# Half of w_v goes through DRAM, the other half is narrowed in place with its steps spread out

## The chip, the cores and the metric

The kernel runs on one core of one Trainium2 chip. The time is device time in microseconds (us). The engines are named as the profile names them: PE is TensorE, DVE is VectorE, ACT is ScalarE, POOL is GpSimd, SP is SyncE, whose queue starts most transfers. Three runs of the kernel before took 486.54, 487.22 and 488.26 us; the median is 487.22 us.

## The reference

Three layers follow one another on 2 x 768 tokens of width 512: a retention layer (attention with decay), a mixture of eight experts, and a channel mix. What bears on the change is the last layer and its weights:

```python
def _moe2_ref(x, mu_k, mu_r, w_k, w_v, w_r):
    x_prev = np.concatenate([np.zeros((B, 1, D), dtype=np.float32), x[:, :-1, :]], axis=1)
    xk = mu_k * x + (1.0 - mu_k) * x_prev
    xr = mu_r * x + (1.0 - mu_r) * x_prev
    k = np.maximum(xk @ w_k, 0.0)
    v = k * k @ w_v
    r = 1.0 / (1.0 + np.exp(-(xr @ w_r)))
    return (r * v).astype(np.float32)

    # the inputs: np.sqrt gives a float64 scalar, so the products are float64
    'w_k': np.random.randn(d_model, d_ff).astype(np.float32) * (1.0 / np.sqrt(d_model)),
    'w_v': np.random.randn(d_ff, d_model).astype(np.float32) * (1.0 / np.sqrt(d_ff)),
    'w_r': np.random.randn(d_model, d_model).astype(np.float32) * (1.0 / np.sqrt(d_model))
```

w_k, w_v and w_r reach the kernel as 64-bit floats. The engines work on 32 bits, so the kernel narrows each of them with integer and float operations on the two 32-bit words of each number.

## The kernel before

Every matrix product is made of three: each operand x is cut into a high part (ACT copies it to the rounded type) and a low part (DVE subtracts the high part from x), and `split3` adds high x high, high x low and low x high. So each weight costs one ACT instruction and one DVE instruction before PE can use it (`w_split`, lines 145 to 159).

The kernel has three phases. The retention layer and the routing of tokens come first. Then a loop over the eight experts: `up` (four column groups fp, PE, then ACT and DVE make the parts of the hidden activations hh and hl), `flip` (inputs of the next expert), `down` (two halves of 128 tokens each). After each of four groups of `up` and four of `down` a side function `side_w` runs; its calls are numbered c = 0 to 63, eight per expert. The last expert's second half is `down_last`. Last comes the channel mix over six groups n of 256 tokens: `k_part(n)` (the product with w_k in four groups fp, then relu, square and the parts k2h, k2l), `r_part(n)` (the product with w_r and the sigmoid), `v_part(n)` (the product with w_v, eight row blocks f for each half t of the tokens). In the text, the groups of `k_part` are called fp0 to fp3.

All engines run their own instruction list in the order in which this Python code issues instructions; an instruction that waits holds everything behind it on its engine, the SP queue of transfers too.

`pieces` (lines 122 to 133) is the list of weight pieces in the order of use. A piece is loaded into one of four buffers `raw` by `w_load` when an earlier piece is finished, and cut into parts by `w_split` about four calls later.

The 64-bit weights take one of two ways:

- `narrow` (line 738): for w_k and w_r. Twelve parts of 128 x 512 numbers are read, narrowed in three steps and written to DRAM as 32-bit floats (`wk32`, `wr32`), and later loaded and cut like any other weight. Step one is `narrow_1` (two DVE instructions), step two `narrow_2` (two), step three `narrow_3` (two); before them ACT takes the magnitude (line 723). One step runs at each call of `side_w` for which line 950 lets it. The list `written` holds the write back until the next call.
- `direct` (line 773): for w_v. Its eight row blocks j are loaded as pieces of kind "d", narrowed in the same three steps, and cut at once into the high part (ACT, line 807) and the low part (DVE, line 786). Its steps run from call c = 56 on, up to three places in `k_part(0)`, then in `r_part(0)` and in `k_part(1)` (two steps after each group). `t`, the buffer of the magnitude, exists once.

`first_k` (line 1106) also makes the inputs of group 1 after fp2: `weigh(1)` on ACT scales the rows, `fetch(1)` transposes them on PE and copies them on ACT (line 1020), `mix(1, 0)` blends them on ACT and DVE (lines 913, 917, 925, 926) for `k_part(1)`; after `r_part(0)`, `mix(1, 1)` makes the same for `r_part(1)`.

Of the kernel before, what the change touches and what calls it, by code (L numbers as in the profile page):

```python
# [10 lines left out]
F32 = mybir.dt.float32  # L11
# [5 lines left out]
ALU = mybir.AluOpType  # L17
# [4 lines left out]
P = 128  # L22
B, H, S, D = 2, 8, 768, 64
DM = H * D
NE, FF = 8, 1024
# [4 lines left out]
ND = DM // P  # L30
NF = FF // P
# [13 lines left out]
def kernel(  # L45
# [16 lines left out]
    act, dve, pool, pe, sp = nc.scalar, nc.vector, nc.gpsimd, nc.tensor, nc.sync  # L62
# [6 lines left out]
    dp = ctx.enter_context(tc.tile_pool(name="dp", bufs=1, space=DRAM))  # L69
# [38 lines left out]

    wk32 = dp.tile([P, ND, FF], F32, name="wk32")
    wr32 = dp.tile([P, ND, DM], F32, name="wr32")
    wpools = [wp1, wp1]

    def w_tiles(kind, i, n, f):
        pl, bufs = (wp1, 2) if kind == "w1" else (wpools[i % 2], 1)
        if (kind, i) == ("w1", NE + 1):
            n *= 2
        return [pl.tile([P, n, f], F32R, name=f"{kind}{x}{i}", tag=f"{kind}{x}", bufs=bufs) for x in "hl"]

    W = {}
    plan = []
    for e in range(NE):
        plan += [("w1", e, w1[e], ND, FF), ("w2", e, w2[e], NF, DM)]
    plan += [("w1", NE, wk32, ND, FF), ("w1", NE + 1, wr32, ND, DM)]
    PIECE = 1024
    pieces = []
    for kind, i, src, n, f in plan:
        m = PIECE // f
        if i == NE + 1:  # L130
            pieces += [("d", NE, wv, NF, DM, j, 1) for j in range(2)]
        pieces += [(kind, i, src, n, f, j, m) for j in range(0, n, m)]
    pieces += [("d", NE, wv, NF, DM, j, 1) for j in range(2, NF)]
    staged = {}
    at = [0, 0]

    def w_load():
        if at[0] < len(pieces):
            kind, i, src, n, f, j, m = pieces[at[0]]
            t = stp.tile([P, m, f], mybir.dt.int64 if kind == "d" else F32, name=f"raw{at[0]}", tag="raw")  # L140
            sp.dma_start(out=t, in_=src[:, j : j + m, :])
            staged[at[0]] = t
            at[0] += 1
# [473 lines left out]
    with ExitStack() as bctx:  # L617
# [120 lines left out]
        def narrow():  # L738

            n = DM  # L740
            parts = []
            for src, dst in ((wk, wk32), (wr, wr32)):
                sv, dv = (x.rearrange("p a b -> p (a b)") for x in (src, dst))
                parts += [(sv[:, j : j + n], dv[:, j : j + n]) for j in range(0, sv.shape[1], n)]
            raws, ts = {}, {}

            def read(k):
                if k < len(parts):
                    raws[k] = bp.tile([P, n], mybir.dt.int64, name=f"raw64_{k}", tag="raw64")
                    sp.dma_start(out=raws[k], in_=parts[k][0])  # L750

            def begin(k):
                if k < len(parts):
                    ts[k] = tp.tile([P, n], I32, name="t1", tag="t1")
                    magnitude(raws[k], ts[k])

            read(0)
            read(1)
            yield
            begin(0)  # L760
            for k in range(len(parts)):
                t2 = tp.tile([P, n], I32, name="t2", tag="t2")
                narrow_1(ts[k])
                yield
                narrow_2(raws[k], ts[k], t2, ts[k])
                yield
                narrow_3(raws[k], ts[k].bitcast(F32), ts[k].bitcast(F32), t2, t2.bitcast(F32))
                written.append(lambda t=t2, k=k: sp.dma_start(out=parts[k][1], in_=t.bitcast(F32)))
                begin(k + 1)
                read(k + 2)  # L770
                yield

        def direct():

            hi, lo = W["w2", NE] = w_tiles("w2", NE, NF, DM)
            todo = [i for i, x in enumerate(pieces) if x[0] == "d"]
            raws, ts = {}, {}
            split = None

            def begin(i):  # L780
                raws[i] = staged.pop(i).rearrange("p a b -> p (a b)")
                ts[i] = tp.tile([P, DM], I32, name="t", tag="t", bufs=1)
                magnitude(raws[i], ts[i])

            def finish(h, l, x):
                dve.tensor_tensor(out=l, in0=x, in1=h.bitcast(F32), op=ALU.subtract)  # L786
                w_load()

            begin(todo[0])
            yield  # L790
            for k, i in enumerate(todo):
                while at[1] < i:
                    w_split()
                    yield
                raw, t = raws[i], ts[i]
                low, high = (raw.bitcast(F32).rearrange("p (n t) -> p n t", t=2)[:, :, x] for x in range(2))
                h, l = (x[:, pieces[i][5], :] for x in (hi, lo))
                narrow_1(t)
                if split:
                    finish(*split)  # L800
                yield

                narrow_2(raw, t, t, high.bitcast(I32))
                yield
                narrow_3(raw, high, low, t, high)
                at[1] += 1
                act.copy(out=h, in_=high)  # L807
                split = h, l, high
                if k + 1 < len(todo):
                    begin(todo[k + 1])  # L810
                yield
            finish(*split)

        conv = narrow()
        perm = bp.tile([P, 2, 2 * P], F32R, name="perm", bufs=1)
# [126 lines left out]
        tail = direct()  # L942

        def side_w():
            c = calls[0]
            calls[0] += 1
            late = list(written)
            if c < 56:
                w_split(1 if c > 1 else 2)
            if c == 2 or (c >= 4 and c % 8 not in (3, 7)):  # L950
                next(conv, None)
            if c >= 56:
                for _ in range((2, 2, 2, 1, 1, 1, 2, 2)[c - 56]):
                    next(tail)
            for w in late:
                w()
            del written[: len(late)]
# [15 lines left out]
    with ExitStack() as mctx:  # L973
# [6 lines left out]
        todo = [(b, g) for b in range(B) for g in range(NG)]  # L980
# [128 lines left out]
        def first_k(fp):  # L1109
            if fp == 0:  # L1110
                mix_first(1, 1)
                x_new(1)
                for a in range(2):
                    act.copy(out=xt[1][:, 2 * a : 2 * a + 2, 0:1], in_=px[1 + a][:, :, GS - 1 : GS])
            else:
                next(tail, None)
            if fp == 1:
                weigh(1)
            if fp == 2:
                fetch(1)  # L1120
                xk[1] = mix(1, 0)
                read(2)

        def two(_):
            for _ in range(2):
                next(tail, None)


        xk, xr = {0: x0[0]}, {}
# [1 line left out]
        pk = k_begin(xk[0])  # L1131
        xr[0] = x0[1]
        k_part(0, xk[0], pk, first_k)
        r_part(0, xr[0], two)
        xr[1] = mix(1, 1)
        k_part(1, xk[1], {}, two)
        for _ in tail:
            pass
        for n in range(1, NN):
# [63 lines left out]
```

## Time and profile before

| | |
|---|---|
| median of three runs | 487.22 us |
| the profiled execution: its time | 489.27 us |
| the profiled execution: its span | 487.5 us |
| PE busy | 453.8 us (93% of the span) |
| DVE busy | 315.7 us (65%) |
| ACT busy | 220.1 us (45%) |
| moved by DMA | 81.86 MB, mean 168 GB/s |

The span runs from the first to the last instruction; the time of the execution is 1.8 us longer. A busy PE is not PE at its peak: PE can be busy at the lower of its two clocks. The line PEclk of the page gives, in 40 slices of the span (12.2 us each), the clock that was granted, in tenths of full speed.

### The profile page before, as it was taken

What the parts mean: (1) busy time and instruction counts of PE and PEld (TensorE: products, weight loads), DVE (VectorE), ACT (ScalarE), POOL (GpSimd) and SP (SyncE); (2) the same over time, 40 slices, a digit from 0 to 9 for tenths busy, and PEclk for the clock granted to TensorE, in tenths of its full rate; (3) what the DMA queues carried; (4) which work ended last, traced back from release to release, by engine and by line L of the source; (5) the groups of instructions that cost most, each with busy time, mean ns of one, the idle gap of its engine ahead of it and who ended that gap; (6) DMA issues with size and microseconds to landing.
All of it is one profiled execution on the core that took longest, in us unless ns stands there. A gap on an engine that the chain in (4) does not pass through costs nothing.

```text
span 487.5 us, 8125 instructions
## 1 busy us (share of the span) xinstructions
PE 453.8 (93%) x3163; PEld 398.8 (82%) x3163; DVE 315.7 (65%) x591; ACT 220.1 (45%) x356; POOL 92.1 (19%) x118
## 2 busy tenths in 40 slices
PE   6999999989999999999999787965899999999997
PEld 4877767969898989898989677953699898989986
DVE  6878866767999696969665867667434363543401
ACT  2133323556647364646453336653444463544300
POOL 3778733502231204231000100000000000000000
PEclk9999999989999999999999898978699999999999
DMA  7998934597999988998681532100200202000011
GB/s 263 390 403 267 291 121 131 171 303 264 371 299 332 310 275 240 331 305 280 213 260 66 185 118 87 42 2 1 65 23 7 81 0 87 1 22 24 0 44 43
DMA packets 27813, 81.86 MB, mean 168 GB/s; under 512 B 4207, under 2 KB 4987, under 8 KB 27772
## 3 DMA queue, kind: packets, MB, share of 16 engines
q1 hardware_dynamic: 23708, 70.30, 43.4%
q0 software_dynamic: 2624, 8.39, 4.7%
q10 hardware_dynamic: 1440, 2.62, 1.4%
q8 instruction: 25, 0.41, 0.3%
q14 instruction: 16, 0.13, 0.1%
HBM read 67.14 MB, written 14.16 MB: 167 GB/s over the span
## 4 chain that ended last, share of the span: by engine, by line
PE 63%; DVE 11%; ACT 4%; DMA 3%; issue 2%; DVEq 0%; ACTq 0%; SPq 0%
PE ps_y L639 6%; PE ps_y L640 5%; PE ps_y L641 5%; PE ps_h L640 5%; PE ps_h L641 5%; PE ps_h L639 5%; PE ps_v L639 4%; PE ps_v L640 4%; PE ps_v L641 4%; PE ps_k L1035 3%; PE ps_k L1034 3%; PE ps_k L1041 3%; DMA xs<-X_n,gidx 2%; PE ps_r L640 2%; PE ps_r L639 2%
## 5 line engine op out<-in xcount | busy, mean ns | idle before, releaser
L640 PE MATMUL ps_h<-xsTl,w1h 128*128 128x256 f32 x256 | 72.8, 284 | 0.1
L639 PE MATMUL ps_h<-xsTh,w1h 128*128 128x256 f32 x256 | 72.7, 284 | 0.0
L641 PE MATMUL ps_h<-xsTh,w1l 128*128 128x256 f32 x256 | 72.4, 283 | 0.0
L639 PE MATMUL ps_y<-w2h,hh 128*128 128x512 f32 (+1 forms) x136 | 53.6, 394 | 0.0
L640 PE MATMUL ps_y<-w2l,hh 128*128 128x512 f32 (+1 forms) x136 | 52.6, 387 | 0.0
L641 PE MATMUL ps_y<-w2h,hl 128*128 128x512 f32 (+1 forms) x136 | 52.5, 386 | 0.0
L157 DVE TENSOR_TENSOR w1l<-raw,w1h 128x1024 fp32r<-128x1024 f32 x38 | 47.8, 1267 | 4.5 <-ACT w1h L156 4.4
L640 PEld LDWEIGHTS ps_h<-xsTl,w1h 128*128 128x128 f32 x256 | 49.0, 192 | 0.9 <-DVE xsTl L175 0.5
L639 PEld LDWEIGHTS ps_h<-xsTh,w1h 128*128 128x128 f32 x256 | 49.0, 192 | 0.5
L641 PEld LDWEIGHTS ps_h<-xsTh,w1l 128*128 128x128 f32 x256 | 49.1, 192 | 0.0
L710 POOL DMA_INDIRECT Y_n<-y,sidx x16 | 20.1, 1258 | 141.4 <-ACT y L700 73.3
L639 PE MATMUL ps_v<-w2h,k2h 128*128 128x512 f32 (+1 forms) x104 | 40.2, 387 | 5.0 <-ACT w2h L807 5.0
L157 DVE TENSOR_TENSOR w2l<-raw,w2h 128x1024 fp32r<-128x1024 f32 x32 | 40.2, 1258 | 7.1 <-ACT w2h L156 6.6
L640 PE MATMUL ps_v<-w2l,k2h 128*128 128x512 f32 (+1 forms) x104 | 40.0, 384 | 3.5 <-DVE w2l L786 3.5
L156 ACT CAST w1h<-raw 128x1024 fp32r<-128x1024 f32 x38 | 39.0, 1052 | 2.6 <-DMA raw<-in_w_dram 2.6
L641 PE MATMUL ps_v<-w2h,k2l 128*128 128x512 f32 (+1 forms) x104 | 39.5, 380 | 0.0
L917 DVE SCALAR_TENSOR_TENSOR t<-xt,mus,t 128x256 f32<-128x256 f32 x40 | 17.6, 480 | 32.1 <-ACT t L913 32.1
L654 DVE SCALAR_TENSOR_TENSOR hl<-ps_h,hh 128x512 fp32r<-128x512 f32 x32 | 21.9, 686 | 23.6 <-ACT hh L653 19.9
L156 ACT CAST w2h<-raw 128x1024 fp32r<-128x1024 f32 x32 | 33.4, 1043 | 4.6 <-DMA raw<-in_w_dram 4.6
L653 ACT ACTIVATE hh<-ps_h 128x512 fp32r<-128x512 f32 x32 | 19.1, 598 | 36.0 <-PE ps_h L641 34.5
L1102 DVE TENSOR_TENSOR o<-ps_v,sg 128x512 f32<-128x512 f32 (+1 forms) x13 | 8.4, 648 | 34.9 <-PE ps_v L641 34.9
L641 PEld LDWEIGHTS ps_y<-w2h,hl 128*128 128x128 f32 x136 | 26.2, 192 | 5.5
(214 smaller groups left out, 1034.3 us busy)
## 6 DMA issues: line engine op xcount, KB each, us to landing
raw<-in_w_dram SPq DMA_DIRECT2D x64, 512.0 KB, 5.5
kv<-in_kv_dram SPq DMA_DIRECT2D x12, 512.0 KB, 8.5
qk<-in_qk_dram SPq DMA_DIRECT2D x11, 512.0 KB
raw<-in_wk_dram SPq DMA_DIRECT2D x8, 512.0 KB, 6.6
raw<-in_wv_dram SPq DMA_DIRECT2D x8, 512.0 KB, 3.5
out_dram<-o SPq DMA_DIRECT2D x11, 256.0 KB
X_n<-xn ACTq DMA_DIRECT2D x10, 256.0 KB
xg<-Y_n SPq DMA_DIRECT2D x10, 256.0 KB, 3.0
```

Of the source, the lines that this page charges most:

```text
L156: act.copy(out=hi[:, j : j + m, :], in_=t)
L157: eng.tensor_tensor(out=lo[:, j : j + m, :], in0=t, in1=hi[:, j : j + m, :].bitcast(F32), op=ALU.subtract)
L639: pe.matmul(ps, wh, xh, start=first, stop=False)
L640: pe.matmul(ps, wh, xl, start=False, stop=False)
L641: pe.matmul(ps, wl, xh, start=False, stop=last)
L653: act.activation(out=hh, in_=ps, func=AF.Relu)
L654: dve.scalar_tensor_tensor(out=hl, in0=ps, scalar=0.0, in1=hh.bitcast(F32), op0=ALU.max, op1=ALU.subtract)
L710: pool.indirect_dma_start(out=Y_n[:, :], out_offset=bass.IndirectOffsetOnAxis(ap=sidx[:, t, e : e + 1], axis=0), in_=y, in_offset=None)
L917: dve.scalar_tensor_tensor(out=m[:, j, :], in0=new(j), scalar=mus[:, i, d : d + 1], in1=t[:, j, :], op0=ALU.mult, op1=ALU.add)
L1034: pe.matmul(ps[:, j, :], wkh[:, d, f], x[0][:, d, :], start=j == d == 0, stop=False, skip_group_check=True)
L1035: pe.matmul(ps[:, j, :], wkl[:, d, f], x[0][:, d, :], start=False, stop=False, skip_group_check=True)
L1041: pe.matmul(ps[:, j, :], wkh[:, d, f], x[1][:, d, :], start=False, stop=d == ND - 1, skip_group_check=True)
```

## The change

Four of the eight row blocks of w_v (j = 0 to 3) join w_k and w_r in `narrow`: they are the last four of sixteen parts, written to the DRAM tile `wv32` and loaded as two pieces of 128 x 1024, cut by `w_split`. The other four (j = 4 to 7) stay in `direct`. `narrow` gets a step at every call from c = 4 on. In `direct` one step now does both `narrow_1` and `narrow_2`, and the high part of a block is issued at the beginning of the step after its `narrow_3`, the low part one step later still. The steps of `direct` run once at each of the calls c = 56 to 61, after fp1 and fp2 of `k_part(0)`, after the second half of `r_part(0)`, and once after each group of `k_part(1)`; one is left for the end. `fetch(1)` and `mix(1, 0)` come after fp3 of `k_part(0)` instead of fp2.

```diff
+    NV = NF // 2
     wk32 = dp.tile([P, ND, FF], F32, name="wk32")
     wr32 = dp.tile([P, ND, DM], F32, name="wr32")
+    wv32 = dp.tile([P, NV, DM], F32, name="wv32")
...
-        if (kind, i) == ("w1", NE + 1):
+        if i >= NE and n < NF and kind + str(i) != f"w1{NE}":
             n *= 2
...
-    plan += [("w1", NE, wk32, ND, FF), ("w1", NE + 1, wr32, ND, DM)]
+    plan += [("w1", NE, wk32, ND, FF), ("w2", NE, wv32, NV, DM), ("w1", NE + 1, wr32, ND, DM)]
...
         if i == NE + 1:
-            pieces += [("d", NE, wv, NF, DM, j, 1) for j in range(2)]
+            pieces += [("d", NE, wv, NF, DM, NV, 1)]
         pieces += [(kind, i, src, n, f, j, m) for j in range(0, n, m)]
-    pieces += [("d", NE, wv, NF, DM, j, 1) for j in range(2, NF)]
+    pieces += [("d", NE, wv, NF, DM, j, 1) for j in range(NV + 1, NF)]
...
-            for src, dst in ((wk, wk32), (wr, wr32)):
+            for src, dst in ((wk, wk32), (wr, wr32), (wv, wv32)):
...
-            def finish(h, l, x):
-                dve.tensor_tensor(out=l, in0=x, in1=h.bitcast(F32), op=ALU.subtract)
-                w_load()
+            def high_part(i):
+                if i in part:
+                    h, l, x = part[i]
+                    act.copy(out=h, in_=x)
+
+            def low_part(i):
+                if i in part:
+                    h, l, x = part[i]
+                    dve.tensor_tensor(out=l, in0=x, in1=h.bitcast(F32), op=ALU.subtract)
+                    w_load()
 
-            begin(todo[0])
-            yield
+            last = None
             for k, i in enumerate(todo):
                 while at[1] < i:
                     w_split()
+                    if at[1] == todo[0]:
+                        begin(todo[0])
                     yield
...
+                high_part(last)
                 narrow_1(t)
-                if split:
-                    finish(*split)
-                yield
                 narrow_2(raw, t, t, high.bitcast(I32))
                 yield
                 narrow_3(raw, high, low, t, high)
                 at[1] += 1
-                act.copy(out=h, in_=high)
-                split = h, l, high
+                part[i] = h, l, high
                 if k + 1 < len(todo):
                     begin(todo[k + 1])
+                low_part(last)
+                last = i
                 yield
-            finish(*split)
+            high_part(last)
+            yield
+            low_part(last)
...
-            if c == 2 or (c >= 4 and c % 8 not in (3, 7)):
+            if c == 2 or c >= 4:
                 next(conv, None)
             if c >= 56:
-                for _ in range((2, 2, 2, 1, 1, 1, 2, 2)[c - 56]):
+                if c < 62:
                     next(tail)
...
-            else:
+            if fp in (1, 2):
                 next(tail, None)
             if fp == 1:
                 weigh(1)
-            if fp == 2:
+            if fp == NF // 2 - 1:
                 fetch(1)
                 xk[1] = mix(1, 0)
                 read(2)
...
-        r_part(0, xr[0], two)
+        r_part(0, xr[0], tail_1)
         xr[1] = mix(1, 1)
-        k_part(1, xk[1], {}, two)
+        k_part(1, xk[1], {}, tail_2)
```

`tail_1` takes a step of `direct` after the second half, `tail_2` after every group; `two` took two steps each time.

The instruction list of ACT in the last expert, before, from the relu of the fourth group of `up` on. L807 is the high part of a block of w_v, L723 the magnitude of the next, L156 the high parts of w_r, L885 the rows of the last expert that go straight to the channel mix:

```order
L653 ACTIVATE hh_3_3225<-ps_h_3_3200 128x512
L807 CAST w2h_3121<-raw_3052 128x512
L723 ACTIVATE t<-raw_3196 128x512
L156 CAST w1h_3252<-raw_3070 128x1024
L156 CAST w1h_3252<-raw_3088 128x1024
L700 COPY y_0_3276<-ps_y_0_3234 128x512
L885 ACTIVATE ylh<-y_0_3276,pslot 128x512
L807 CAST w2h_3121<-raw_3196 128x512
L723 ACTIVATE t<-raw_3256 128x512
L885 ACTIVATE ylh<-ps_y_10_3283,pslot 128x256
```

The same place now (line numbers are higher by 2 at first, by 10 later; L725 is the magnitude, L158 the high part of a weight piece):

```order
L655 ACTIVATE hh_3_3270<-ps_h_3_3245 128x512
L725 ACTIVATE t<-raw_3208 128x512
L158 CAST w1h_3296<-raw_3137 128x1024
L158 CAST w1h_3296<-raw_3174 128x1024
L702 COPY y_0_3320<-ps_y_0_3278 128x512
L895 ACTIVATE ylh<-y_0_3320,pslot 128x512
L895 ACTIVATE ylh<-ps_y_10_3327,pslot 128x256
```

Both high parts of w_v and one magnitude have left this place.

ACT in `k_part(0)`, before, from the scaling of group 1's rows (L1001) to the blend of them (L913, L925); L1070 and L1071 are relu and square of a group:

```order
L1001 ACTIVATE xg_3409<-xg_3409,pe_p 128x512 x2
L1070 ACTIVATE rl<-ps_k_3422 128x512
L1071 ACTIVATE k2h_3543<-rl 128x512
L807 CAST w2h_3121<-raw_3256 128x512
L723 ACTIVATE t<-raw_3272 128x512
L1020 COPY xt_3503<-ps_t_3555 128x4x128
L1020 COPY xt_3503<-ps_t_3561 128x4x128
L913 ACTIVATE t_3567<-xt_3503,mus_103 128x256 x2
L925 CAST w1h_3252<-t_3568 128x512
```

The same place now (L789 is the high part of a block of w_v):

```order
L789 CAST w2h_3170<-raw_3121 128x512
L1011 ACTIVATE xg_3436<-xg_3436,pe_p 128x512 x2
L1080 ACTIVATE rl<-ps_k_3449 128x512
L1081 ACTIVATE k2h_3573<-rl 128x512
L725 ACTIVATE t<-raw_3300 128x512
L1080 ACTIVATE rl<-ps_k_3585 128x512
L1081 ACTIVATE k2h_3611<-rl 128x512
L1030 COPY xt_3530<-ps_t_3618 128x4x128
L1030 COPY xt_3530<-ps_t_3624 128x4x128
L923 ACTIVATE t_3630<-xt_3530,mus_103 128x256 x2
L935 CAST w1h_3296<-t_3631 128x512
```

The relu and square of fp3 now stand ahead of the copies of group 1, and the magnitude ahead of them waits for the single buffer `t`, which DVE frees with `narrow_3` of the block before.

DVE at the end of `k_part(1)`, before, from the low part of the seventh block of w_v to the first output (L1073, L1074 make the square and its low part, L1102 the output):

```order
L786 TENSOR_TENSOR w2l_3122<-raw_3323,w2h_3121 128x512
L731 SCALAR_TENSOR_TENSOR t<-raw_3622,t 128x512
L732 TENSOR_SCALAR raw_3622<-t 128x512
L1073 TENSOR_TENSOR sq<-rl 128x512
L1074 TENSOR_TENSOR k2l_3828<-sq,k2h_3827 128x512
L735 SCALAR_TENSOR_TENSOR raw_3622<-raw_3622 128x512
L736 TENSOR_TENSOR raw_3622<-raw_3622,t 128x512
L786 TENSOR_TENSOR w2l_3122<-raw_3622,w2h_3121 128x512
L1102 TENSOR_TENSOR o<-ps_v_3839,sg 128x512
```

The same place now, over the last two groups:

```order
L1083 TENSOR_TENSOR sq<-rl 128x512
L1084 TENSOR_TENSOR k2l_3803<-sq,k2h_3802 128x512
L737 SCALAR_TENSOR_TENSOR raw_3316<-raw_3316 128x512
L738 TENSOR_TENSOR raw_3316<-raw_3316,t 128x512
L794 TENSOR_TENSOR w2l_3171<-raw_3300,w2h_3170 128x512
L1083 TENSOR_TENSOR sq<-rl 128x512
L1084 TENSOR_TENSOR k2l_3839<-sq,k2h_3838 128x512
L794 TENSOR_TENSOR w2l_3171<-raw_3316,w2h_3170 128x512
L1112 TENSOR_TENSOR o<-ps_v_3848,sg 128x512
```

Behind the last square only one low part is left, where a whole third step and the low part stood.

## Rows read from the trace of the kernel before

**Rows 1.** The page's second part: PE's granted clock in 40 slices, in tenths.

```profile
PEclk9999999989999999999999898978699999999999
```

**Rows 2.** Busy time by stretch: PE, PEld, DVE, ACT, POOL, then PEclk, DMA share, GB/s.

```profile
125.06:148.63 23.57, 23.57 (x154) 21.39 (x153) 21.92 (x36) 13.39 (x19) 4.75 (x5) 1.00 0.95 338
...
267.00:285.00 18.00, 12.70 (x68) 10.92 (x66) 14.45 (x28) 6.29 (x11) 1.60 (x1) 0.91 0.49 160
285.00:348.60 63.60, 47.46 (x287) 42.76 (x288) 43.51 (x81) 33.48 (x65) 1.49 (x5) 0.84 0.14 44
348.60:487.50 138.90, 135.75 (x813) 121.26 (x812) 53.35 (x92) 54.38 (x101) 0.39 (x2) 1.00 0.09 32
```

**Rows 3.** Instructions in order of time, PE: start, us, line, count, idle before.

```profile
276.88 1.30 PE L874 MATMUL ps_f<-ident,xg__3238 128*128 128x128 f32 x4 [2.91 <-DVE xg__3238 L860]
...
283.45 0.38 PE L892 MATMUL ps_f<-perm,ylh 128*128 128x256 f32 x1 [1.14 <-ACT ylh L885]
285.01 0.38 PE L892 MATMUL ps_f<-perm,yll 128*128 128x256 f32 x1 [1.18 <-DVE t L909]
...
299.88 1.27 PE L1019 MATMUL ps_t<-ident,xg 128*128 128x128 f32 x8 [2.82 <-ACT xg L1001]
...
310.82 0.28 PE L1034 MATMUL ps_k<-w1h,w1h 128*128 128x256 f32 x1
...
313.69 0.28 PE L1034 MATMUL ps_k<-w1h,w1h 128*128 128x256 f32 x1
...
324.48 0.58 PE L1034 MATMUL ps_k<-w1h,w1h 128*128 128x256 f32 x1 [4.87 <-ACT rl L1070]
...
329.19 0.40 PE L639 MATMUL ps_v<-w2h,k2h 128*128 128x512 f32 x1
...
339.17 0.80 PE L640 MATMUL ps_v<-w2l,k2h 128*128 128x512 f32 x1 [3.46 <-DVE w2l L786]
...
345.38 1.91 PE L1019 MATMUL ps_t<-ident,xg 128*128 128x128 f32 x8
```

**Rows 4.** Instructions in order of time, ACT, from the last expert to the sigmoid.

```profile
266.69 0.60 ACT L653 ACTIVATE hh<-ps_h 128x512 fp32r<-128x512 f32 x1 [0.22 <-PE ps_h L641]
...
273.00 1.98 ACT L156 CAST w1h<-raw 128x1024 fp32r<-128x1024 f32 x2
...
281.83 0.65 ACT L807 CAST w2h<-raw 128x512 fp32r<-128x512 f32 x1 [5.61 <-DVE raw L736]
...
299.12 1.32 ACT L1001 ACTIVATE xg<-xg,pe_p 128x512 f32<-128x512 f32 x2
...
305.02 1.07 ACT L1020 COPY xt<-ps_t 128x512 f32<-128x512 f32 x2
...
309.81 0.62 ACT L925 CAST w1h<-t 128x512 fp32r<-128x512 f32 x1 [0.74 <-DVE t L917]
...
311.61 1.28 ACT L1086 ACT_TABLE_LOAD   x1
```

**Rows 5.** Instructions in order of time, DVE: a square pair, then one block of w_v.

```profile
311.07 0.68 DVE L1073 TENSOR_TENSOR sq<-rl 128x512 f32<-128x512 f32 x1
...
312.47 0.42 DVE L727 TENSOR_SCALAR t<-t 128x512 f32<-128x512 f32 x1
...
313.26 0.68 DVE L786 TENSOR_TENSOR w2l<-raw,w2h 128x512 fp32r<-128x512 f32 x1
313.87 0.69 DVE L731 SCALAR_TENSOR_TENSOR t<-raw,t 128x512 int32<-128x512 int32 x1
...
315.05 0.70 DVE L735 SCALAR_TENSOR_TENSOR raw<-raw 128x512 f32<-128x512 uint32 x1
315.78 0.69 DVE L736 TENSOR_TENSOR raw<-raw,t 128x512 f32<-128x512 f32 x1
```

**Rows 6.** Transfers: issues by line, size, median us from issue to landing.

```profile
raw<-in_wk_dram SPq DMA_DIRECT2D x8, 512.0 KB, 6.6
...
wr<-t SPq DMA_DIRECT2D x4, 256.0 KB, 5.3
```

More of the change, by code (lines that the diff above doesn't have):

```diff
@@ L741, in narrow @@
             parts = []
-            for src, dst in ((wk, wk32), (wr, wr32)):
+            for src, dst in ((wk, wk32), (wr, wr32), (wv, wv32)):
                 sv, dv = (x.rearrange("p a b -> p (a b)") for x in (src, dst))
-                parts += [(sv[:, j : j + n], dv[:, j : j + n]) for j in range(0, sv.shape[1], n)]
+                parts += [(sv[:, j : j + n], dv[:, j : j + n]) for j in range(0, dv.shape[1], n)]
             raws, ts = {}, {}
@@ L773, in direct @@
         def direct():
-            hi, lo = W["w2", NE] = w_tiles("w2", NE, NF, DM)
             todo = [i for i, x in enumerate(pieces) if x[0] == "d"]
             raws, ts = {}, {}
-            split = None
+            part = {}
             def begin(i):
@@ L796, in direct @@
                 low, high = (raw.bitcast(F32).rearrange("p (n t) -> p n t", t=2)[:, :, x] for x in range(2))
-                h, l = (x[:, pieces[i][5], :] for x in (hi, lo))
+                h, l = (x[:, pieces[i][5], :] for x in W["w2", NE])
+                high_part(last)
                 narrow_1(t)
-                if split:
-                    finish(*split)
-                yield
                 narrow_2(raw, t, t, high.bitcast(I32))
@@ L1122, in first_k, with tail_1, tail_2 @@
                 read(2)
-        def two(_):
-            for _ in range(2):
+        def tail_1(t):
+            if t:
                 next(tail, None)
+        def tail_2(_):
+            next(tail, None)
         xk, xr = {0: x0[0]}, {}
```

## The prediction

> **What bounds the kernel now.** I read the granted clock over the span first. It is 9 tenths or more almost everywhere and falls to 6 to 8 tenths, after one early slice, only in slices 22, 24 and 26 to 28 (counted from 0, 12.2 us each), that is between 268 and 353 us [rows 1]. Then the busy time by stretch: in an expert PE is busy for all of its 23.57 us, and after 348.6 us for 135.75 of 138.90 us, so neither place has much to give. Between 267 and 348.6 us PE is busy for 12.70 + 47.46 = 60.16 of 81.6 us: 21.4 us idle, at a mean clock of 0.91 and 0.84 [rows 2]. Third, PE's instructions in order of time, to find what ended each idle stretch: the rows of the first expert product that go on to the channel mix, the scaling of group 1's rows, a relu on ACT, and at last the parts of w_v on DVE [rows 3]. Fourth, ACT and DVE over the same stretch: the high part of w_v waits 5.61 us on ACT for the narrowing on DVE, with everything behind it on ACT waiting too [rows 4]. So the end is set here by two in-order queues, ACT and DVE, that wait for each other, with PE behind both.
>
> There are two prices to pay for an idle PE: the wait, and the clock after it. The last group of k_part(1) comes after 4.87 us of idling and takes 329.19 - 324.48 = 4.71 us; the same 24 products take 313.69 - 310.82 = 2.87 us when PE was busy before [rows 3]. The first is largely at 1.2 GHz, the second at 2.4 GHz. I take 1.8 us of slow clock behind every wait near 3 us or longer; after the two waits of 1.14 and 1.18 us I take none.
>
> **Part 1, four blocks move into the expert loop.** One block costs DVE, start to start, 0.79 us for step one (312.47 to 313.26), 1.18 for step two (313.87 to 315.05), 1.42 for step three (315.05 to the end at 316.47) and 0.61 for the low part (313.26 to 313.87): 4.00 us in all [rows 5]. Narrowing now has eight steps per expert instead of six, so 2 x 3.39 / 3 = 2.3 us more DVE work. The fullest expert holds 21.92 of 23.57 us [rows 2], so it would want 24.2: 0.6 us too much, once. A late low part of the hidden activations is missed only in `down`, a call (23.57 / 8 = 2.9 us) or more later, and weight pieces are cut a whole expert ahead; PE hides it, and I take 0. If each of six experts passed 0.6 us on it would be 3.6 us; a gain is excluded, since PE has no idle time there to lose. Transfers grow by 2/3 of a part per expert, 512 KB read and 256 KB written: 0.52 MB in 23.57 us, 22 GB/s on 338 at a share of 0.95 [rows 2]. That expert would be at its limit. Weight loads are issued four calls, 11.8 us, ahead, and a load takes 6.6 us [rows 6], so I take 0 here too. The two pieces of the half that went through DRAM are cut at c = 56 and 57 in two instructions per piece: nothing new, because a whole narrowing stood in the same calls.
>
> **Part 2, the first wait.** Before, ACT's two high parts of w_r start at 273.00 us because a high part of w_v and a magnitude stood in front [rows 4]; DVE's low parts and the scaling of the gathered rows come behind them, and PE waits 2.91 us [rows 3]. Now only the magnitude of the second block precedes them. It needs the buffer `t`, free after step three of the first block: the fourth relu starts at 266.69 [rows 4] as before and takes 0.6, DVE's low part of it 0.6 and step three 1.4 come behind, so at 269.3 us. Magnitude 0.6, two high parts 2.0 [rows 4], then 1.2 for the second low part and 0.9 for the scaling: 274.1 us instead of 277.1. PE comes there at 276.88 - 2.91 = 273.97. Gain 2.8, and 1.8 of clock.
>
> **Part 3, the next two waits.** 1.14 and 1.18 us: PE waits for the weighted rows, which stood on ACT behind the high part that waited 5.61 us [rows 3, 4]. No step of `direct` is left at c = 62 and 63, so both go: gain 2.3. Running sum 6.9 us; from here to the group fp2 the lists of ACT and DVE are alike, and everything keeps this shift.
>
> **Part 4, fetch after fp3.** PE now has fp3 (2.9 us) to do while ACT scales group 1. The scaling began at 299.12 [rows 4], minus 6.9 is 292.2, plus 0.6 for a high part put in front; the first half is done at 293.5, while PE ends fp3 at 299.88 - 2.82 - 6.9 + 2.9 = 293.1. The wait of 2.82 shrinks to about 0.5, and the slow clock goes: gain 2.3 + 1.8. Sum 11.0; `r_part(0)` ends at 310.82 - 11.0 = 299.8.
>
> **Part 5, what is late next.** Here the change adds a wait. ACT's magnitude of the third block stands ahead of fp3's relu and of the copies for mix(1, 0), and waits for step three of the block before. DVE: free at about 293.1 (a high part and a low part of fp1 behind the anchor at 292.2), steps one and two 1.97, a square pair 1.40 (311.07 to 312.47), step three 1.42 [rows 5]: 297.9. ACT: magnitude, relu, square, 0.6 each: copies start at 299.7. From their start the first half of the blend takes 3.2 and the second 309.81 + 0.62 - 305.02 = 5.4 us [rows 4]: 302.9 and 305.1. PE stands ready at 299.8 and waits 3.1 us, goes slow (1.8), and waits a little for the second half: fp0 of `k_part(1)` ends near 308, the next three at 2.87 each near 316.6. Before, it was 329.19 [rows 3]: sum 12.6. The 4.87 us wait and its slow clock are gone, and 4.9 + 0.2 of it is given back earlier.
>
> **Part 6, the end of w_v.** ACT after 305.1: the table of the sigmoid 1.28 [rows 4], two sigmoids and a high part 1.6, the blend mix(1, 1) 4.2 (the 5.4 without its copies): 312.1, and DVE's last blend instruction ends near 312.8. Then DVE alone decides: pair 1.40, step three 1.42, low part of the second block 0.61, a wait of about 0.5 for the relu and square behind the last magnitude, pair 1.40, steps one and two 1.97, pair 1.40, step three 1.42, low part of the third 0.61: 323.5. Pair 1.40 and the last low part 0.61: 325.5. PE begins `v_part(0)` at 316.6, uses the first six blocks and one product (19 x 0.23 = 4.4 us) until 321.0, waits 2.5 for the third block's low part, then about 1 for the last one, and ends its first half near 326.7 with the clock down, as it is down before. Before, it ended at 345.38 [rows 3]. Sum 18.7 us. Behind it nothing changes.
>
> **The sum against its own time.** The profiled execution took 489.27 us, span 487.5 and 1.77 around it; 489.27 - 18.7 = 470.6. It is 2.05 us above the median of the runs, 487.22, so the median should come to 468.5 us. The errors: parts 5 and 6 are chains of some twenty steps, 2 us either way; each slow clock of 1.8 us may be missing or come once more; part 1 may cost up to 3.6.
>
> **Rivals.**
>
> *The gain is only the DVE work that leaves.* Eight blocks and two pieces of w_r, 8 x 4.00 + 2 x 1.2, become four blocks and four pieces, 4 x 4.00 + 4 x 1.2: 13.6 us, so 473.6. For it: DVE does the last thing that PE waits for. Against it: DVE is busy for only 14.45 + 43.51 of 81.6 us there [rows 2]; much of the loss is waiting.
>
> *The round trip is late.* The last part is written to DRAM at c = 52, behind 1.3 us of step three, near 250 us; the load of its piece must wait for the write, 5.3 us, and takes up to 6.6 [rows 6]: 262.0, where ACT wants it at 261.4. If both took 3 us more, the first wait would stay (2.8 + 1.8): 473. The Trainium skill, "DMA: Bandwidth & Descriptors", section Rules for kernel authors, says that a DMA that reads what another wrote must wait for the first one's completion before it is issued. By that rule SP, in order, also holds the next loads of w_v and w_r meanwhile; no run here shows yet for how long.
>
> *All waits go.* If the chains of parts 5 and 6 are shorter than I add them, what remains is the clock-free work: 21.4 us of idling and about 4 x 1.8 of slow clock leave, 28.6, so 458.6. Against it: mix(1, 0) was moved later, and it is needed right after `r_part(0)`.
>
> *Slower: the raw loads of the narrowing hold ACT.* A part is read three calls, 8.8 us, before its magnitude now (before, 11.8 on the average), and ACT waits for it in order, with the relu of `up` behind. If a load takes L, PE loses L - 8.8 at each of some 15 parts, once 5.8 us (two spare groups in PSUM) are used up. It eats the 18.7 us from L = 8.8 + 24.5 / 15 = 10.4 us on; at 11 us it is 33 - 5.8 - 18.7 = 8.5 us slower, 495.7. The row says 6.6 [rows 6], at a share that is to rise to 1.
>
> **How the numbers follow.** My forecast, 465 to 472 us: 0.64. DVE work only, 0.15; late round trip, 0.09; all waits gone, 0.07; slower, 0.04; none of them, 0.01. The range of 464 to 475 leaves out the full gain, the slower case and half of the tails of the second. A measurement of this kernel tells about 0.3% (1.5 us) from no change. Faster by more 0.95, within it 0.01, slower 0.04.
>
> **What would show it.** Right: PE's wait before the rows of the channel mix below 0.5 us; none at the two weighted products; 0.5 us before group 1's transposes; a new wait of about 3 us at the start of `k_part(1)`, ended by the blend on ACT; about 2.5 us and 1 us in `v_part(0)`, ended by low parts of w_v on DVE; PE idle between 267 us and the end of that stretch near 8 us instead of 21.4; experts of 23.57 us as before. Wrong: experts that grow, ACT waiting for raw loads there, or a wait at the first of w_r's high parts.

## The result, and the profile after

The changed kernel took 468.57 us (median of four runs, 466.59 to 472.78); the kernel before, on the same chip, 487.74 (486.54 to 488.59). The ratio is 0.962, 95% interval 0.954 to 0.970. The forecast was 468.5 us, range 464 to 475. Runs of one kernel lie up to 6 us apart, so agreement to 0.1 us is partly luck; what the trace says of each step is the better test.

The profiled execution is the longest of the four: 472.78 us, span 471.1. The page's row of the granted clock, after:

```profile
PEclk8899997899999999999999999989999999999999
```

Of the low slices 22, 24 and 26 to 28 of [rows 1], one is left, slice 26 at 8 tenths. Slices 0, 1, 6 and 7 are new: they lie ahead of everything that the change moves, and come back at the end of this document.

To compare the same work in both, I cut a window between two places that both programs have: the last transposes of an expert's inputs (`flip(7)`), and the first transposes of group 2, which stand behind the first half of `v_part(0)`. Columns as in [rows 2]; first before:

```profile
242.87:345.38 102.51, 81.07 (x499) 72.61 (x497) 71.28 (x126) 49.25 (x87) 5.03 (x8) 0.90 0.28 91
```

and after, with an expert and the rest:

```profile
125.06:148.63 23.57, 23.57 (x153) 21.34 (x153) 22.36 (x37) 12.21 (x19) 6.40 (x5) 1.00 0.89 320
...
246.15:329.43 83.28, 76.12 (x498) 68.90 (x497) 60.13 (x102) 46.50 (x81) 4.76 (x8) 0.97 0.33 105
...
329.40:471.00 141.60, 138.41 (x825) 123.81 (x823) 54.08 (x93) 56.12 (x104) 0.38 (x2) 0.99 0.10 34
```

I call this window the tail. It shrank from 102.51 to 83.28 us: 19.23. PE's idle time in it went from 102.51 - 81.07 = 21.44 to 7.16 us (14.28 less), and the same products took 76.12 instead of 81.07 us (4.95 less), at a granted clock of 0.97 instead of 0.90. The expert still takes 23.57 us with PE busy throughout. The stretch behind the tail is 142.12 us before (487.5 - 345.38) and 141.67 after. The last expert starts 3.28 us later (246.15 against 242.87), and 3.28 - 19.23 - 0.45 = -16.4 us is the difference of the spans.

PE's waits after, in order of time:

```profile
277.08 0.91 PE L884 MATMUL ps_f<-ident,xg__3282 128*128 128x128 f32 x4
...
296.25 1.27 PE L1029 MATMUL ps_t<-ident,xg 128*128 128x128 f32 x8 [0.50 <-ACT xg L1011]
...
305.64 0.39 PE L1044 MATMUL ps_k<-w1h,w1h 128*128 128x256 f32 x1 [2.64 <-ACT w1h L935]
...
307.81 0.58 PE L1044 MATMUL ps_k<-w1h,w1h 128*128 128x256 f32 x1 [0.95 <-ACT w1h L935]
...
311.32 0.28 PE L1044 MATMUL ps_k<-w1h,w1h 128*128 128x256 f32 x1
...
319.94 0.40 PE L641 MATMUL ps_v<-w2h,k2h 128*128 128x512 f32 x1
...
326.42 0.50 PE L642 MATMUL ps_v<-w2l,k2h 128*128 128x512 f32 x1 [1.97 <-DVE w2l L794]
...
328.42 0.80 PE L642 MATMUL ps_v<-w2l,k2h 128*128 128x512 f32 x1 [1.04 <-DVE w2l L794]
...
329.43 1.91 PE L1029 MATMUL ps_t<-ident,xg 128*128 128x128 f32 x8
```

The waits of 2.91, 1.14 and 1.18 us of [rows 3] are gone (a row without a bracket did not wait), 2.82 became 0.50, and 4.87 and 3.46 gave way to two pairs, 2.64 and 0.95 at the start of `k_part(1)`, 1.97 and 1.04 in `v_part(0)`. Two more waits of before, not in [rows 3], are gone too; they were for high parts of w_v on ACT:

```profile
335.20 0.51 PE L639 MATMUL ps_v<-w2h,k2h 128*128 128x512 f32 x1 [1.74 <-ACT w2h L807]
...
343.64 0.80 PE L639 MATMUL ps_v<-w2h,k2h 128*128 128x512 f32 x1 [3.24 <-ACT w2h L807]
```

With them PE waited 8.44 us for w_v in `v_part(0)` before. ACT's rows tell why the first new pair is there:

```profile
272.59 0.67 ACT L725 ACTIVATE t<-raw 128x512 f32<-128x512 f32 x1 [2.08 <-DVE raw L738]
273.17 1.98 ACT L158 CAST w1h<-raw 128x1024 fp32r<-128x1024 f32 x2
...
300.63 0.68 ACT L725 ACTIVATE t<-raw 128x512 f32<-128x512 f32 x1 [2.67 <-DVE raw L738]
...
304.97 0.62 ACT L935 CAST w1h<-t 128x512 fp32r<-128x512 f32 x1 [0.55 <-DVE t L927]
```

The magnitude of the third block waits 2.67 us for the one buffer `t`, and the blend that PE wants (L935) stands behind it on ACT.

### The profile page after: what moved, and what is told of

It reads as the page before. It is cut to its first block, busy times and chain, and to the rows that moved or that the text cites. A ratio compares the mean times of both kernels' runs of the same rounds, so it can differ in the third digit from the quotient of the medians.

```text
span 471.1 us, 8147 instructions
## 1 busy us (share of the span) xinstructions
PE 453.2 (96%) x3163; PEld 399.3 (85%) x3163; DVE 314.5 (67%) x589; ACT 219.4 (47%) x354; POOL 92.1 (20%) x118
## 4 chain that ended last, share of the span: by engine, by line
PE 55%; DVE 14%; ACT 5%; DMA 4%; issue 3%; DVEq 0%; SPq 0%; ACTq 0%
PE ps_v L642 4%; PE ps_v L643 4%; PE ps_v L641 4%; PE ps_y L643 4%; PE ps_h L642 4%; PE ps_y L641 4%; PE ps_y L642 4%; PE ps_h L643 4%; PE ps_h L641 4%; PE ps_k L1045 3%; PE ps_k L1044 3%; PE ps_k L1051 3%; DMA raw<-in_wk_dram 3%; DVE w2l L159 2%; PE ps_r L642 2%
## 5 line engine op out<-in xcount | busy, mean ns | idle before, releaser
L159 DVE TENSOR_TENSOR w2l<-raw,w2h 128x1024 fp32r<-128x1024 f32 x34 | 42.7, 1254 | 6.5 <-ACT w2h L158 6.2
L158 ACT CAST w1h<-raw 128x1024 fp32r<-128x1024 f32 x38 | 39.1, 1052 | 5.6 <-DMA raw<-in_w_dram 5.6
L158 ACT CAST w2h<-raw 128x1024 fp32r<-128x1024 f32 x34 | 35.6, 1048 | 5.7 <-DMA raw<-in_w_dram 5.7
L927 DVE SCALAR_TENSOR_TENSOR t<-xt,mus,t 128x256 f32<-128x256 f32 x40 | 17.6, 480 | 30.7 <-ACT t L923 30.7
L725 ACT ACTIVATE t<-raw 128x512 f32<-128x512 f32 x20 | 13.6, 679 | 35.9 <-DMA raw<-in_wk_dram 17.4
L642 PEld LDWEIGHTS ps_y<-w2l,hh 128*128 128x128 f32 x136 | 25.6, 189 | 5.1
```

Of the source, the lines that this page charges most:

```text
L158: act.copy(out=hi[:, j : j + m, :], in_=t)
L159: eng.tensor_tensor(out=lo[:, j : j + m, :], in0=t, in1=hi[:, j : j + m, :].bitcast(F32), op=ALU.subtract)
L642: pe.matmul(ps, wh, xl, start=False, stop=False)
L725: act.activation(out=t.bitcast(F32), in_=words(raw)[2], func=AF.Abs)
L927: dve.scalar_tensor_tensor(out=m[:, j, :], in0=new(j), scalar=mus[:, i, d : d + 1], in1=t[:, j, :], op0=ALU.mult, op1=ALU.add)
```

## The experiments

Beside the time I give each kernel's tail, measured between the same two places in its one profiled execution. Each ratio is to runs of the kernel before on the same chip. The chip is not the same for all experiments, so they are compared with each other by ratio and by tail, not by their times.

### One place earlier for the fetch

```diff
-            if fp == NF // 2 - 1:
+            if fp == 2:
                 fetch(1)
```

> The changed kernel with fetch(1) and mix(1, 0) back after fp2 of k_part(0); all else as changed. Theory of two queues (ACT and DVE set the end, PE's waits only move): PE waits about 3.3 us before group 1's transposes again and then runs slow for 1.8 us, but the wait at the start of k_part(1) goes, and the last low part of w_v ends only about 0.6 us later: 468 to 471 us. Rival, that each wait of PE counts by itself: 2.3 + 1.8 us come back, about 472.7 us.

471.18 us, ratio 0.965 (0.959 to 0.971). PE:

```profile
295.16 1.27 PE L1029 MATMUL ps_t<-ident,xg 128*128 128x128 f32 x8 [3.37 <-ACT xg L1011]
...
325.36 0.50 PE L642 MATMUL ps_v<-w2l,k2h 128*128 128x512 f32 x1 [3.26 <-DVE w2l L794]
```

The old wait for the scaling is back, with 3.37 us, and the 2.64 at `k_part(1)` is gone; the tail is 83.29 us (245.08 to 328.37), as after the change. So this edit is worth nothing by itself: DVE's last low part of w_v ends 82.22 us after the start of the tail, against 82.21 in the changed kernel, and PE waits for it at one place or at another. Counting each wait by itself would have made the tail some 4 us longer. The time does not separate the two (472.7 of 487.22 us is a ratio of 0.970, inside the interval); the tail does.

### The order alone, and the half alone

The change has two parts, so I ran each without the other. First the new order of steps with all eight blocks of w_v in `direct`. Eight blocks need twice as many steps as four, so here two steps stand at each of the calls 56 to 58 and after three groups of `k_part(1)`, and one after each half of `r_part(0)`; the order is not quite that of the change:

```diff
-                for _ in range((2, 2, 2, 1, 1, 1, 2, 2)[c - 56]):
+                for _ in range((2, 2, 2, 1, 1, 1, 0, 0)[c - 56]):
...
+                high_part(last)
+                narrow_1(t)
                 narrow_2(raw, t, t, high.bitcast(I32))
...
+                low_part(last)
+                last = i
```

> The kernel before with the new order of steps alone: all eight blocks of w_v in place, nothing more through DRAM; high part one step after, low part two, steps one and two together, none of them at c = 62 and 63, fetch after fp3. Theory of two queues: the two weighted products no longer wait (2.3 us) and the wait before the transposes shrinks (4 us), but DVE has all eight blocks to do, the first wait grows by about 1.6 us, and the end is DVE's chain: 479 to 485 us. Rival, that the gain is the DVE work that leaves: none leaves, 487 us.

486.18 us, ratio 0.994 (0.991 to 0.996), less than I expected. Its tail, and PE's waits in it:

```profile
244.27:344.32 100.05, 83.05 (x499) 73.46 (x498) 72.13 (x126) 49.37 (x87) 4.39 (x8) 0.88 0.28 93
```

```profile
274.60 0.50 PE L641 MATMUL ps_y<-w2h,hl 128*128 128x512 f32 x1 [1.94 <-DVE hl L654]
281.50 1.04 PE L883 MATMUL ps_f<-ident,xg__3247 128*128 128x128 f32 x4 [2.40 <-DVE xg__3247 L869]
...
302.21 1.27 PE L1028 MATMUL ps_t<-ident,xg 128*128 128x128 f32 x8 [0.50 <-ACT xg L1010]
...
311.60 0.39 PE L1043 MATMUL ps_k<-w1h,w1h 128*128 128x256 f32 x1 [2.64 <-ACT w1h L934]
313.76 0.58 PE L1043 MATMUL ps_k<-w1h,w1h 128*128 128x256 f32 x1 [0.95 <-ACT w1h L934]
...
335.14 0.79 PE L640 MATMUL ps_v<-w2l,k2h 128*128 128x512 f32 x1 [3.85 <-DVE w2l L793]
336.94 0.79 PE L639 MATMUL ps_v<-w2h,k2h 128*128 128x512 f32 x1 [0.58 <-ACT w2h L788]
...
341.29 0.79 PE L640 MATMUL ps_v<-w2l,k2h 128*128 128x512 f32 x1 [3.56 <-DVE w2l L793]
343.30 0.80 PE L640 MATMUL ps_v<-w2l,k2h 128*128 128x512 f32 x1 [0.36 <-DVE w2l L793]
```

DVE has as much to do as before (72.13 against 71.28 us). The waits in the middle do shrink: those of 1.14 and 1.18 us are gone, and 2.82 became 0.50. But at the end PE waits for w_v as long as before (3.85 + 0.58 + 3.56 + 0.36 = 8.35 us against 8.44), and a wait of 1.94 us is new in the last expert, where steps one and two stand on DVE ahead of the low part of a hidden activation. PE's idle time falls by 4.4 us, to 17.0; its products take 2.0 us longer (83.05 against 81.07) at a granted clock of 0.88 instead of 0.90, and 2.5 us are left as gain.

Then half of w_v through DRAM, but the old steps of `direct`, the old calls and the fetch after fp2:

```diff
-                if c < 62:
+                for _ in range((2, 2, 2, 1, 1, 1, 2, 2)[c - 56]):
                     next(tail)
...
-                part[i] = h, l, high
+                act.copy(out=h, in_=high)
+                split = h, l, high
```

> The changed kernel with the old order of steps: half of w_v through DRAM, but direct() with the old steps at the old places and fetch after fp2. Theory of two queues: about 1.5 us of the first wait stays, the waits before the weighted products and before the transposes stay, w_v is ready before k_part(1) ends and the waits in v_part(0) go: 470 to 474 us. Rival, that the gain is the DVE work that leaves: 473.6 us, with the first waits gone. Rival, that the order is what counts: 485 us or more.

476.04 us, ratio 0.974 (0.969 to 0.978), again less of a gain than I expected. Its tail and its two longest waits:

```profile
242.71:332.58 89.87, 78.29 (x498) 71.49 (x497) 59.97 (x102) 46.37 (x81) 4.90 (x8) 0.92 0.30 97
```

```profile
277.87 0.48 PE L875 MATMUL ps_f<-ident,xg__3289 128*128 128x128 f32 x1 [3.22 <-DVE xg__3289 L861]
...
304.59 1.97 PE L1020 MATMUL ps_t<-ident,xg 128*128 128x128 f32 x8 [6.24 <-ACT xg L1002]
```

DVE is relieved as in the full change (59.97 against 60.13 us), and PE no longer waits for w_v at the end; but ACT and DVE still wait for each other in the middle: ahead of the scaling that PE waits 6.24 us for, ACT's high part of w_v waits 2.22 us for DVE, and behind it DVE waits 2.98 us for a relu on ACT. The tails: order alone 2.5 us shorter, half alone 12.6, both 19.2, which is 4.1 more than the sum. The two help each other. The rows fit this reading: the order alone leaves the waits for w_v at the end, the half alone leaves the waits in the middle. That nothing else is in the 4.1 us is not shown.

### A second buffer t

```diff
-                ts[i] = tp.tile([P, DM], I32, name="t", tag="t", bufs=1)
+                ts[i] = tpools[(len(ts) + 1) % len(tpools)].tile([P, DM], I32, name="t", tag="t", bufs=1)
...
+        tpools.append(mp)
```

> The changed kernel with a second buffer t for the magnitude of the third block of the four (in the pool of the channel mix). Theory of two queues: that magnitude no longer waits for DVE (2.67 us on ACT), fp3's relu and the copies of group 1 come 2.7 us earlier, DVE's chain lets 1.5 us of it through, and the waits at the start of k_part(1) fall from 3.6 to about 2: 1.5 to 3 us faster than the changed kernel, 465.5 to 467 us. Rival, that DVE alone sets that stretch: no change, 468.5 us.

467.99 us, ratio 0.954 (0.948 to 0.960); tail 81.00 us (244.33 to 325.33), 2.3 shorter.

```profile
302.27 0.39 PE L1047 MATMUL ps_k<-w1h,w1h 128*128 128x256 f32 x1 [1.09 <-ACT w1h L937]
...
322.31 0.50 PE L642 MATMUL ps_v<-w2l,k2h 128*128 128x512 f32 x1 [2.72 <-DVE w2l L796]
```

The wait of 2.64 us was made by the single buffer for 1.55 of it, so DVE alone does not set this stretch: its chain begins when ACT lets it. At the end PE waits longer for w_v (2.72 instead of 1.97), which takes back 0.7 us: DVE's low parts still close the tail.

### Less for DVE at the end: a step earlier, and six blocks

If DVE's chain at the end decides, then moving work from it to an earlier place must shorten the tail by about that work. One step of the second block moved into an idle stretch of DVE (with the second `t`):

```diff
-                if c < 62:
+                if c < 63:
```

> The changed kernel with a second buffer t, and one more step of direct at call c = 62, so that every later step of direct comes one place earlier. Theory (at the end the in-order work of DVE decides when the last low part of w_v is there): steps one and two of the second block, 1.97 us, fill an idle stretch of 2.02 us of DVE before the second low part of the last expert's rows and leave the chain behind it; the length from the first transposes of the last expert to those of v_part(0), 83.3 us in the changed kernel and 81.0 with the second t alone, comes to 79 to 80; the time to 464.5 to 467 us, ratio to before 0.947 to 0.953. Rival (the rows of the last expert are just as urgent on DVE, and what is taken away behind is given back there): a new wait of 1 to 2 us before the weighted products or k_part(0), length 81 to 83, time 467 to 470.

465.72 us, ratio 0.950 (0.946 to 0.954); tail 79.49 us (243.61 to 323.10), 1.5 shorter than with the second `t` alone, for 1.97 us of work moved. The step's four instructions end at 278.0, and the low part behind them waits for nothing:

```profile
277.61 0.43 DVE L734 TENSOR_SCALAR raw<-t 128x512 int32<-128x512 int32 x1
278.07 0.48 DVE L898 SCALAR_TENSOR_TENSOR yll<-ps_y,pslot,ylh 128x256 fp32r<-128x256 f32 x1
```

Six of the eight blocks through DRAM, from the changed kernel (one buffer `t`):

```diff
-    NV = NF // 2
+    NV = 6
...
+    pieces += [("w2", NE, wv32, NV, DM, 4, 2)]
...
             high_part(last)
+            w_split()
             yield
```

> The changed kernel with six of eight blocks of w_v through DRAM instead of four, the third of their pieces cut at the end, and two blocks in direct. Theory (DVE's work in the tail decides): two blocks of 4.00 us leave and one low part of 1.2 us comes, 6.8 us; the waits of 2.64 and 0.95 us in k_part(1) and of 1.97 and 1.04 us in v_part(0) go for the most part, length of the tail 76.5 to 79 instead of 83.3, experts stay at 23.6 us; time 461 to 465 us, ratio 0.945 to 0.953. Rival 1 (the raw loads of two more parts, now up to c = 57, hold ACT and so PE): the experts grow, the time is 468 us or more. Rival 2 (the mix of group 1 is the bound and not the parts of w_v): the wait of 2.64 us stays, tail 80 to 82, time 465.5 to 467.5.

463.71 us, ratio 0.948 (0.945 to 0.951); tail 77.88 us (242.63 to 320.51). PE waits for w_v no more; 0.50 us for the scaling, 1.09 and 0.95 for the blend and 1.3 for a relu remain. The experts did not grow (six in 242.63 - 100.83 = 141.80 us). DVE's work in the tail hardly changed:

```profile
242.63:320.51 77.88, 73.94 (x498) 67.29 (x497) 59.24 (x101) 46.22 (x80) 6.03 (x8) 1.00 0.37 124
```

The six steps of the two further blocks run at the calls 52 to 57, which lie inside the tail, near its start. So the 5.4 us were won by the place of DVE's work and not by its amount (59.24 against 60.13 us). The same holds for the step moved above (59.86 against 59.85). Last, the step of two blocks that stood in front of that blend on DVE, behind it:

```diff
-            if fp in (1, 2):
+            if fp == 1:
...
                 xk[1] = mix(1, 0)
+                next(tail, None)
```

> The kernel with six blocks through DRAM, and the step of direct that stood after fp2 of k_part(0) (step three of the last block and the low part of the one before, 2.0 us on DVE) now behind the blend mix(1, 0). Theory (what is left in the tail is set by DVE's blend for k_part(1), which starts 2.0 us late behind that step): the wait of 1.09 us at the start of k_part(1) goes, that of 0.95 us may stay, nothing comes back in v_part(0), the tail is 76 to 77.3 us instead of 77.9, the time 461.5 to 463.5 us, ratio 0.944 to 0.948. Rival (the blend waits for the transposed rows as well, so ACT's copies are the bound): tail 77.5 to 78.5, time as with six blocks, 463 to 464.5.

460.71 us (459.65 to 464.88), ratio 0.944 (0.940 to 0.948), the shortest of all; its interval overlaps that of six blocks alone, and its tail is 1.8 us shorter. Tail, and the two waits left beside 0.50 us for the scaling:

```profile
242.09:318.17 76.08, 73.66 (x498) 67.35 (x497) 59.32 (x101) 46.23 (x80) 6.09 (x8) 1.00 0.37 126
```

```profile
300.47 0.38 PE L1046 MATMUL ps_k<-w1h,w1h 128*128 128x256 f32 x1 [0.52 <-ACT w1h L937]
...
309.73 0.39 PE L1046 MATMUL ps_k<-w1h,w1h 128*128 128x256 f32 x1 [1.34 <-ACT rl L1082]
```

PE is idle for 2.42 us, at a granted clock of 1.00. So 73.66 us is what the tail's products take at 2.4 GHz, and the 81.07 of before held 7.4 us of slow clock.

### The raw loads of the narrowing, one and two calls later

The prediction priced at nothing that ACT waits for raw loads in the experts, and named it the slower rival. The profile after does show such waits: 28.8 us ahead of the magnitudes in six experts (5.9 before), 22.8 of them for raw loads. I issued each raw load later, by one call (the first diff) and by two (the same behind `narrow_2`):

```diff
                 narrow_1(ts[k])
+                if k:
+                    read(k + 1)
                 yield
...
                 begin(k + 1)
-                read(k + 2)
```

> The changed kernel with every raw load of the narrowing (from the third part on) issued one call later, so two calls (5.9 us) before its magnitude instead of three (8.8 us). Theory (ACT has some 11 us of idle time in an expert, PE has two spare groups in PSUM, 5.8 us, and what ACT loses at one part it has made up by the next): a load lands after 5.8 to 6.9 us, ACT waits more but PE does not, experts stay under 23.8 us, time 466 to 472 us, no difference from the changed kernel. Rival (the slower case of the prediction: PE loses the load's time minus the lead at each of some 15 parts, less 5.8 us once): 15 x (6.9 - 5.9) - 5.8 = 9 us more, 475 to 480.

> The same with the raw loads issued only one call (2.9 us) before the magnitude. Theory (waits of ACT are covered up to 5.8 us each and do not add up): ACT waits up to 4 us per part, PE little: experts at most 24.1 us, time 468 to 475 us. Rival (they add up): 15 x (6.9 - 2.9) - 5.8 = 54 us more, 515 to 525; in between, 490 to 500, if ACT's waits are made up only by half.

491.08 us, ratio 1.005 (1.003 to 1.008), and 533.1 us, ratio 1.093 (1.087 to 1.099). My theory for both fell. The page's row of the magnitudes (busy, mean ns, idle before them with its chief cause), and six experts as one window, in the changed kernel:

```profile
L725 ACT ACTIVATE t<-raw 128x512 f32<-128x512 f32 x20 | 13.6, 679 | 35.9 <-DMA raw<-in_wk_dram 17.4
```

```profile
103.81:246.15 142.34, 142.03 (x913) 128.45 (x914) 128.95 (x186) 84.51 (x117) 30.78 (x24) 1.00 0.93 316
```

the same with the loads one call later, with what PE waited for in the experts (us, times, longest):

```profile
L725 ACT ACTIVATE t<-raw 128x512 f32<-128x512 f32 x20 | 13.4, 672 | 83.4 <-DMA raw<-in_wk_dram 33.4
```

```profile
99.93:259.88 159.95, 147.67 (x913) 130.84 (x913) 125.36 (x180) 78.96 (x112) 31.28 (x24) 0.98 0.83 273
```

```profile
PE ps_h L641 <- DVE hl L656: 7.1, 3, 3.4
PE ps_y L643 <- DVE hl L656: 3.5, 3, 1.2
PE ps_y L641 <- ACT hh L655: 1.6, 2, 1.0
```

and two calls later:

```profile
103.03:299.20 196.17, 159.87 (x912) 139.81 (x913) 123.76 (x179) 77.42 (x110) 31.11 (x24) 0.89 0.67 218
```

ACT's idle time ahead of the magnitudes grows from 35.9 to 83.4 us over the whole run. In the six experts it grows from 28.8 to 69.7 (104.7 with two calls less), nearly all of it for raw loads. Then PE waits for the parts of the hidden activations, which stand behind the magnitude on ACT, and for the PSUM buffers that their making frees (`ps_h`). The experts grow by 17.6 us (12.0 more idle, 5.6 more for the same products, at a granted clock of 0.98 instead of 1.00) and by 53.8 us (36.0 and 17.8, at 0.89). The rival's formula, 15 times the load's time less the lead, less 5.8 us, gave 9 and 54 us more than the changed kernel; against the kernel before on each chip the changes are 21.7 and 63.7 us. It is too low; the rows show that a late part delays the next loads as well. SP and one magnitude of the kernel with one call less:

```profile
132.98 8.03 SPq L143 DMA_DIRECT2D raw<-in_w_dram  x3
141.06 0.45 SPq L752 DMA_DIRECT2D raw<-in_wk_dram  x1
```

```profile
148.24 0.66 ACT L725 ACTIVATE t<-raw 128x512 f32<-128x512 f32 x1 [7.57 <-DMA raw<-in_wk_dram]
```

The raw load is issued at 141.06, behind three weight loads that held SP's queue for 8.03 us, and its magnitude starts 7.2 us later. A weight load needs a buffer that DVE's low part frees, behind ACT's high part, behind the magnitude that waits: a ring through SP, ACT and DVE. Over the six experts, the waits of SP's weight loads that the profile puts down to DVE's step one (L729), which itself needs the magnitude, add up to 34.2 us in the changed kernel (the longest 4.2), 64.4 with one call less (8.3) and 99.7 with two (9.9). That the ring makes up the whole of the excess is argued from these rows, not shown.

## Why the prediction was right

*Part 1, cost 0.* Right: six experts took 142.34 us (143.05 before between the same places), PE idle 0.3 of it. DVE's work in them grew by 1.8 us per expert (117.99 to 128.95 over six, 2.3 forecast), and the transfers by 22 GB/s, as forecast (294 to 316). But one of my signs of being wrong came: ACT did wait there for raw loads, which I had taken as covered, and only PE did not feel it. The cover is thin. With one call less of lead, 2.9 us, the whole gain was gone. The chance of 0.04 for that rival was fair only if the lead was sure; I put the load at 6.6 us against a lead of 8.8 and should have said that 2.2 us was all that stood between 468 and some 490.

*Parts 2 and 3.* Right: the waits of 2.91, 1.14 and 1.18 us left. The magnitude in front had to wait for the buffer `t`, as I had it: 2.08 us on ACT, 2.0 forecast. The high parts of w_r start at 273.17, in an execution whose last expert began 3.28 us later, so 3.1 us earlier in the program than before, as forecast (269.9 against 273.00).

*Part 4.* The forecast was 0.5 us and the trace has 0.50. But the fetch one place earlier gave the same tail. So the 2.3 + 1.8 us credited to this step are not its own: the gain belongs to DVE's chain, and the step only chose where PE waits.

*Part 5.* Right in place and cause (ACT's magnitude behind the one `t`), 2.64 + 0.95 us against about 3.1 and a little.

*Part 6.* Right: the third block's low part after 1.97 us (forecast 2.5), the last one after 1.04 (about 1), both from DVE:

```profile
325.68 0.68 DVE L794 TENSOR_TENSOR w2l<-raw,w2h 128x512 fp32r<-128x512 f32 x1
...
327.68 0.68 DVE L794 TENSOR_TENSOR w2l<-raw,w2h 128x512 fp32r<-128x512 f32 x1
```

*The sum.* 18.7 us forecast, 19.23 in the tail; idle time near 8 us forecast, 7.16 found. So I had 13.4 us of idling and 5.3 of slow clock, and the trace has 14.28 and 4.95. With the 3.28 us of the later start taken off, the places between came out too: `r_part(0)` ended at 299.7 (299.8 forecast), fp0 of `k_part(1)` at 308.0 (308), its last group at 316.7 (316.6), the last low part of w_v at 325.1 (325.5), the first half of `v_part(0)` at 326.2 (326.7). So the mechanism held step by step; that the median of the runs fell within 0.1 us of the forecast is luck. The execution that was profiled came to 472.78 and not 470.6 because of a slow clock ahead of what the change moves (below).

*The rivals.* "Only the DVE work that leaves" gave 13.6 us. It fits the half alone (12.6), where the old order keeps the mutual waits, and fails for the whole: DVE's busy time in the tail fell by 71.28 - 60.13 = 11.15 us, the tail by 19.23. "All waits go" needed 28.6 us; the best kernel reached 102.51 - 76.08 = 26.4, with two more blocks of DVE's work moved ahead. The late round trip did not happen: no wait stands at the high parts of w_r, nor at those of the two pieces of w_v. SP was held, though: it issued the last write at 253.25 and the load that reads it at 257.82, 4.0 us of that waiting for the write to land. Writes and loads of these parts landed in 4.2 to 4.9 us, less than the 5.3 and 6.6 of the sum, and the high part that needed the load, at 264.65, found it there. The mechanism of the slower one is real, 2.9 us of lead away.

## What to carry to other kernels

When two in-order engines wait for each other and one of them also ends the stretch, sum the work of the one that ends it first: reordering pays only as far as that chain leaves room, and a wait taken away in the middle can come back at its end (with the second `t`, 0.7 of 1.55 us). What counts is where that engine's work stands, as much as how much it is. Compare the parts of a change between two fixed places of the program and split the difference into idle time and slow clock; one window row does both. Before calling work hidden, measure the lead that hides it, in the unit in which the program can lose it (here one call, 2.9 us, was worth 22 us).

## What was not expected of the hardware

*The clock early in the run.* In the profiled execution after, 75 to 85 us was granted 0.54, in a part of the retention layer that both kernels share:

```profile
75.00:85.00 10.00, 10.00 (x50) 7.64 (x50) 3.96 (x16) 2.80 (x6) 2.69 (x3) 0.54 0.38 118
...
305.60:308.00 2.40, 1.41 (x9) 1.21 (x10) 1.70 (x4) 1.64 (x4) 0.00 (x0) 0.96 0.00 0
308.00:311.00 3.00, 3.00 (x15) 3.00 (x16) 2.37 (x5) 2.99 (x5) 0.00 (x0) 0.50 0.00 0
```

The same stretch was granted 1.00 before. An earlier one, 5 to 15 us, was granted 0.66, behind waits of PE for its first loads (the longest 1.90 us); before, 1.00. Behind both, the same work stood 4.90 us later than before; a shorter wait for a gather took 0.91 of it back and the experts 0.71, and 3.28 are left, by which the last expert starts later. The other runs of the changed kernel, 466.59 to 470.39 us, have mean clocks of 0.993 to 0.985 where this one has 0.975. What starts it stays open.

*After a wait.* I took 1.8 us of slow clock behind every wait near 3 us. Behind the wait of 2.64 us the granted clock was 0.96 (305.6 to 308), and it was 0.50 only from 308 to 311, behind the second wait of 0.95. With waits of 1.09 and 0.95 us at the same place (second `t`), the tail's mean clock was 0.99.
